# Attention and a feed-forward layer on one core: float32r scores by 64-row products on two row halves

## The chip, the cores and the metric

The kernel runs on one core of a Trainium2 chip. The metric is the device time of one execution in microseconds. Five engines work side by side, each on its own queue in order: TensorE (PE, with weight loads as PEld), VectorE (DVE), ScalarE (ACT), GpSimd (POOL) and SyncE (SP, which issues most DMAs here). They wait for each other by semaphores.

## The reference

Eight batches of eight heads, 576 positions, 64 lanes a head. Each head's scores get a bias from a running sum, a causal mask and a softmax; then a feed-forward layer runs over the 512 joined lanes of all 4608 tokens. All is float32 (q and k are drawn with a spread of 0.8, v of 0.1, s of 0.5).

```python
scores = (1 / np.sqrt(64)) * np.matmul(q, k.transpose(0, 1, 3, 2))
cum = np.cumsum(np.maximum(s, 0.0), axis=-1)
bias = -(cum[:, :, :, None] - cum[:, :, None, :])
scores = np.where(causal, -1000000000.0, scores + np.minimum(bias, 0.0))
attn = np.exp(scores - max); attn = attn / (sum(attn) + 1e-09)
x = np.matmul(attn, v)            # heads side by side: 4608 x 512
h = x @ w_in                      # 512 x 2048
g = np.where(h >= 1, h, np.where(h <= -1, 0.0, (h + 1) ** 2 / 4))
out = g @ w_out                   # 2048 x 512
```

## The kernel before

**Jobs.** Attention goes in 64 jobs: `jobs` runs over 8 batches, the two halves of the query positions (`HALF`: 320 and 256 positions), and four pairs of heads. A job takes two heads. Its query rows are tiles `QT`: 64, 128 and 128 rows in the first half (tiles 0, 1, 2, which see 64, 192 and 320 keys), 128 and 128 in the second (tiles 3, 4, which see 448 and 576; tile 4 goes in two column halves of 288). `att_slot(j, k)` emits a job in eight slots k. Between the slots the main loop emits `ffn_step`: for each half batch, 16 times twelve h products (`ffn_h`, L594, 128x320 or 128x256, f16) and twelve y products (`ffn_y`, L633). A scheduler then orders each engine's instructions by a model of its own, within the order that data, buffers and priorities ask for; the slots set the rank of the work.

**Scores.** The first 12 jobs (`F32_JOBS`, "whole" jobs) use float32 products (L432). Their operands hold 64 lanes of a head and four more rows: the running sum `cum` in two parts and constants, so that the bias comes out of the product itself (68 rows, `KC`). The 52 jobs from the 13th on (24 first halves, 28 second halves) use float32r, which keeps fewer bits, so each operand is split in two parts. The operands are four tiles, one copy each: `Q1s` and `K1s` have 128 rows, `Q2s` and `K2s` 68. `rq` and `rk` are loaded twice, into rows 0 to 63 and 64 to 127. `att_prep`, at slot 0 of the job itself, lets ACT round them (L387, L388, L389) and DVE subtract (L390, L391), and ACT's queue load `cum`'s parts into `Q2s` and `K2s` (L381, L382). Per tile, head and column half, `scores` then makes a product over 128 rows (L435) and one over 68 rows (L436) into the same bank `s` (pool `ps_s`, two banks, which `px` uses too).

**Behind the scores.** DVE adds the mask and takes the row minimum in one instruction (L441, PSUM to the tile `p`), ACT takes the exponential (L452), DVE the reciprocal of the sum (L494, L495), POOL, ACT and DVE split the weights in two f16 parts `pb` (L499 to L505), and an SP DMA transposes them into `pt`. A job later, `att_out` multiplies them with v (L535, 128 rows by 64 columns, the two heads on the two column halves of the array), and ACT and DVE make the f16 parts of x. Once a batch, L121 spreads a scale: a product with one row and one column of data.

Of the kernel before, what the change touches and what calls it, by code (L numbers as in the profile page):

```python
# [22 lines left out]
P = 128  # L23
# [54 lines left out]
def attention_ffn(ctx: ExitStack, tc: tile.TileContext, qT, kT, vn, s, w_in, w_out, yT):  # L78
# [269 lines left out]
    def att_load(n, hf):  # L348

        b, h0 = n // NPAIR, 2 * (n % NPAIR)  # L350
        q0, N, _ = HALF[hf]
        W = q0 + N
        if whole(n, hf):
            for t, src, c0 in zip(operands(n, hf), (qT, kT), (q0, 0)):
                sv = src[b, h0:h0 + 2, :, c0:W].rearrange("h d n -> d h n")
                (FIRSTQ if jobs.index((n, hf)) < FIRST_N else LOADQ).dma_start(t[:D, :, :W - c0], sv)
            return
        rq = ap.tile([P, 2, N], F32, tag="rq", bufs=1, name=f"rq{n}_{hf}")
        rk = ap.tile([P, 2, W], F32, tag="rk", bufs=1, name=f"rk{n}_{hf}")
# [4 lines left out]
        raws[n, hf] = rq, rk

    def att_prep(n, hf):
# [4 lines left out]
        if not whole(n, hf) and not split_tiles:  # L371
            split_tiles.extend(operand_tiles(F32R, "s"))
            constant_rows(*split_tiles[1])
        Qc, Kc = operands(n, hf) if whole(n, hf) else split_tiles[1]
# [8 lines left out]
        if whole(n, hf):  # L383
            return
# [4 lines left out]
        A.copy(Q2[:D, :, :N], rq[:D])  # L389
        V.tensor_tensor(Q1[D:, :, :N], rq[D:], Q1[D:, :, :N].bitcast(F32), ALU.subtract)  # L390
        V.tensor_tensor(K2[:D, :, :W], rk[:D], K1[:D, :, :W].bitcast(F32), ALU.subtract)  # L391
# [24 lines left out]

    def scores(n, i, hd, c0, c1):

        off, R, W = QT[i]
        qo = off - HALF[i // 3][0]  # L420
        if hd == 0 and c0 == 0:
            sums[n, i] = ap.tile([P, 2], F32, tag="sm", bufs=4, name=f"sm{n}_{i}")
            pbs[n, i] = []
        if c0 == 0:
            Pt = ap.tile([P, SP], F32, tag="p", bufs=4, name=f"p{n}_{i}_{hd}")
            pbs[n, i].append(Pt)
            G.memset(Pt[:R, W:W + D], 0.0)
# [1 line left out]
        sc = ps_s.tile([P, 512], F32, tag="s", name=f"s{n}_{i}_{hd}_{c0}")
        if whole(n, i // 3):  # L430
            Q, K = operands(n, i // 3)
            T.matmul(sc[:R, :c1 - c0], Q[:KC, hd, qo:qo + R], K[:KC, hd, c0:c1], start=True, stop=True)  # L432
        else:
# [1 line left out]
            T.matmul(sc[:R, :c1 - c0], Q1[:, hd, qo:qo + R], K1[:, hd, c0:c1], start=True, stop=False)  # L435
            T.matmul(sc[:R, :c1 - c0], Q2[:KC, hd, qo:qo + R], K2[:KC, hd, c0:c1], start=False, stop=True)  # L436
        mn = mins.pop((n, i, hd), None)
        m2 = ap.tile([P, 1], F32, tag="mn", bufs=6, name=f"mn{n}_{i}_{hd}_{c0}")
        mo = 448 - off + c0
        with tc.high_priority(offset=TTR_LEAD):  # L440
            ttr[0] = V.tensor_tensor_reduce(  # L441
                out=Pt[:R, c0:c1], in0=sc[:R, :c1 - c0], in1=mask[:R, mo:mo + c1 - c0],
                scale=-0.125, scalar=3.0e38 if mn is None else mn[:R],
                op0=ALU.add, op1=ALU.min, accum_out=m2[:R],
            ).ins
# [320 lines left out]
```

## Time and profile before

| | |
|---|---|
| three runs | 1098.88, 1101.65, 1103.4 us, median 1101.65 |
| profiled execution | 1098.98 us, span 1097.2 us, mean granted TensorE clock 0.984 |
| busy PE, PEld | 1014.7 us (92%), 779.6 us (71%) |
| busy DVE, ACT, POOL | 862.9 us (79%), 722.7 us (66%), 657.8 us (60%) |
| score products of the split jobs | L435 118.1 us (x312), L436 96.2 us (x312) |
| DMA | 140.33 MB, 128 GB/s on average |

Times of one instruction run from its start to its modelled end. PE's products overlap: a stream of 320-column products has one every 0.136 us though each lasts 0.30. So a sum of busy times says how long PE was occupied, and the price of a product is read from the starts of its neighbours. "Idle before" is the time that an engine stood still before an instruction, with the one that released it.

### The profile page before, as it was taken

How to read it: one execution, taken by the hardware profiler on the slowest of the kernel's cores; microseconds unless marked ns; L12 is line 12 of the kernel's file. 1: busy time of each engine (PE TensorE's matmuls, PEld its weight loads, DVE VectorE, ACT ScalarE, POOL GpSimd, SP SyncE). 2: the span in 40 equal slices, each digit the busy share in tenths (PEclk: the TensorE clock that was granted, in tenths of full speed). 3: DMA queues.
4: the chain of work that ended last, by engine and by line, in shares of the span. 5: the costliest groups of instructions: out<-in, count | busy, mean ns of one | idle time of the engine just before them, and what ended most of it. 6: DMA issues, size and time to landing. Idle time of an engine off the chain costs nothing. (4 is left out here: it accounts for less than half of the span.)

```text
span 1097.2 us, 25029 instructions
## 1 busy us (share of the span) xinstructions
PE 1014.7 (92%) x8494; PEld 779.6 (71%) x8494; DVE 862.9 (79%) x2379; ACT 722.7 (66%) x1707; POOL 657.8 (60%) x1139
## 2 busy tenths in 40 slices
PE   1567898999999999999999999899999999999998
PEld 0334566687778877787778877787777877887787
DVE  7998986678788878788788778787888888887533
ACT  4867683567567765877577765776577765777432
POOL 2843486666567656666567665666566666765522
PEclk9998999799999999999999999999999999999999
DMA  8835245546357763777366753766276753677300
GB/s 241 240 119 172 77 101 112 124 107 167 92 116 164 133 145 87 161 143 151 88 146 144 160 124 84 160 134 166 71 161 131 154 127 73 153 137 139 68 25 20
DMA packets 300839, 140.33 MB, mean 128 GB/s; under 512 B 237608, under 2 KB 286632, under 8 KB 300712
## 3 DMA queue, kind: packets, MB, share of 16 engines
q1 hardware_dynamic: 291008, 128.80, 52.2%
q10 hardware_dynamic: 9704, 9.93, 3.2%
q8 instruction: 67, 1.10, 0.4%
q14 instruction: 60, 0.49, 0.1%
HBM read 71.00 MB, written 9.73 MB: 74 GB/s over the span
## 5 line engine op out<-in xcount | busy, mean ns | idle before, releaser
L594 PE MATMUL h<-x,WI 128*128 128x256 f16 (+1 forms) x3072 | 461.4, 290 | 11.9 <-DVE u L610 7.8
L633 PE MATMUL y<-g,WO 128*128 128x256 f16 (+1 forms) x3072 | 446.2, 287 | 1.9 <-ACT g L620 1.9
L594 PEld LDWEIGHTS <-WI 128*128 128x128 f16 x3072 | 287.9, 99 | 105.0 <-issue 22.1
L633 PEld LDWEIGHTS <-WO 128*128 128x128 f16 x3072 | 288.0, 98 | 85.4 <-issue 5.7
L621 POOL TENSOR_TENSOR g<-u,g 128x320 f16<-128x320 f32 (+1 forms) x256 | 207.0, 808 | 172.0 <-ACT g L620 164.0
L452 ACT ACTIVATE p<-p,mn 64x64 f32<-64x64 f32 (+4 forms) x320 | 179.4, 561 | 118.3 <-DVE mn L441 84.6
L606 ACT ACTIVATE u<-h,ub,us 128x320 f32<-128x320 f32 (+1 forms) x256 | 149.3, 583 | 131.8 <-PE h L594 130.0
L609 DVE SCALAR_TENSOR_TENSOR h<-h,ws,u 128x320 f32<-128x320 f32 (+1 forms) x256 | 132.8, 519 | 87.7 <-ACT u L606 84.1
L499 POOL TENSOR_SCALAR pb<-p,rs 128x256 f16<-128x256 f32 (+4 forms) x148 | 94.1, 636 | 142.1 <-DVE rs L495 88.7
L502 POOL TENSOR_TENSOR pb<-p,pb 128x256 f16<-128x256 f32 (+4 forms) x148 | 156.0, 1054 | 9.8
L441 DVE CUSTOM_DVE_ANT_0 p<-s,mask 64x64 f32<-64x64 f32 (+4 forms) x320 | 134.8, 422 | 34.2 <-PE s L436 21.6
L505 DVE SCALAR_TENSOR_TENSOR pb<-p,rs,pb 128x256 f16<-128x256 f32 (+4 forms) x148 | 127.8, 864 | 22.3 <-POOL pb L499 21.7
L610 DVE SCALAR_TENSOR_TENSOR u<-u,r,h 128x320 f32<-128x320 f32 (+1 forms) x256 | 130.5, 510 | 7.4
L435 PE MATMUL s<-K1s,Q1s 128*128 128x288 f32 (+4 forms) x312 | 118.1, 379 | 10.1 <-DVE Q1s L390 5.0
L500 ACT ACTIVATE p<-p,rs 128x192 f32<-128x192 f32 (+4 forms) x148 | 84.2, 569 | 51.5 <-DVE rs L495 49.2
L620 ACT CAST g<-u 128x320 f16<-128x320 f32 (+1 forms) x256 | 108.1, 422 | 6.5 <-DVE u L610 6.3
L501 POOL TENSOR_SCALAR pb<-p 128x256 f16<-128x256 f32 (+4 forms) x148 | 87.6, 592 | 16.7 <-ACT p L500 12.6
L436 PE MATMUL s<-K2s,Q2s 68*128 68x288 f32 (+4 forms) x312 | 96.2, 308 | 0.1
L535 PEld LDWEIGHTS <-vt 128*64 128x64 f16 x1464 | 68.5, 112 | 19.9 <-issue 14.0
L535 PE MATMUL px<-pt,vt 128*64 128x256 f16 (+3 forms) x1464 | 77.2, 257 | 2.7 <-DMA pt<-pb 2.6
L435 PEld LDWEIGHTS s<-K1s,Q1s 128*128 128x128 f32 (+1 forms) x312 | 56.7, 182 | 19.5 <-PE s L436 4.5
L391 DVE TENSOR_TENSOR K2s<-rk,K1s 64x1152 fp32r<-64x1152 f32 (+1 forms) x52 | 62.9, 1209 | 5.9 <-ACT K1s L388 5.1
(134 smaller groups left out, 1034.8 us busy)
## 6 DMA issues: line engine op xcount, KB each, us to landing
rk<-in_k_dram SPq DMA_DIRECT2D x56, 288.0 KB
wir<-in_moe_w_in_dram SPq DMA_DIRECT2D x16, 512.0 KB
v<-in_v_dram SPq DMA_DIRECT2D x32, 256.0 KB
wor<-in_moe_w_out_dram SPq DMA_DIRECT2D x16, 512.0 KB
rk<-in_k_dram SPq DMA_DIRECT2D x48, 160.0 KB
rq<-in_q_dram SPq DMA_DIRECT2D x48, 160.0 KB
rq<-in_q_dram SPq DMA_DIRECT2D x56, 128.0 KB
out_dram<-o ACTq DMA_DIRECT2D x32, 160.0 KB
```

The lines of the kernel that those rows point to most:

```text
L435: T.matmul(sc[:R, :c1 - c0], Q1[:, hd, qo:qo + R], K1[:, hd, c0:c1], start=True, stop=False)
L441: ttr[0] = V.tensor_tensor_reduce(out=Pt[:R, c0:c1], in0=sc[:R, :c1 - c0], in1=mask[:R, mo:mo + c1 - c0], scale=-0.125, scalar=3.0e38 if m ...
L452: A.activation(Pt[:R, :W], Pt[:R, :W], AF.Exp, bias=m2[:R], scale=-1.0, accum_out=sums[n, i][:R, hd:hd + 1])
L502: G.tensor_tensor(los[1], pw, his[1], ALU.subtract)
L505: V.scalar_tensor_tensor(los[0], pv, rs[:R, :1], his[0], ALU.mult, ALU.subtract)
L535: T.matmul(px[hd * D:(hd + 1) * D, lo:N], vts[n][:, vl, j, hd * D:(hd + 1) * D], PT[:, 4 * j + 2 * hd + pl, lo:], start=(m == 0), stop=(m ...
L594: T.matmul(h[:, :N], WI[4 * kt + ft // 4][:, wl, ft % 4 * P:(ft % 4 + 1) * P], x[:, kt, xl], start=(n == 0), stop=(n == 3 * NKT - 1),)
L606: first = A.activation(u, h[:, :N], AF.Relu, bias=ubi[b], scale=usc[b]).ins
L609: V.scalar_tensor_tensor(h[:, :N], h[:, :N], wsc[b], u, ALU.mult, ALU.max)
L610: V.scalar_tensor_tensor(u, u, r, h[:, :N], ALU.min, ALU.mult)
L621: G.tensor_tensor(g[:, 1], u, g[:, 0], ALU.subtract)
L633: T.matmul(ys[b, hf, m][:, :N], WO[8 * (m // 2) + ft // 2][:, wl, c0:c0 + P], g[:, gl], start=(ft == 0 and n == 0), stop=(ft == NFT - 1 an ...
```

## The change

From the 13th job on, the two heads of a job lie on rows 0 to 63 and 64 to 127 of one operand tile, so q and k are loaded once. `att_split` makes the high part (ACT, L393 and L394) and the low part (DVE) of q and k at slot 3 of the job before, into one of two sets of tiles in turn. `score_pair` makes three products over 64 rows for each tile and head (high by high, low by high, high by low; L508), alternating between the heads, that is between the upper and the lower row half of the array. It does so for a group of tiles at a time (`PAIRS`): tiles 0 and 1 in one bank, tile 2, tile 3, and tile 4's two halves, hence two groups in a first-half job and three in a second-half job, 132 in all. The running sum no longer goes through the product: `bias_load` spreads `cum` of both heads over all partitions by DMA from ACT's queue (L407), POOL adds the causal mask to the diagonal block (`bias_mask`, L414), and DVE's reduction (now L456) reads that tile in place of the mask. The signs of the constant rows and of `cum` are turned round.

```diff
+PAIRS = (
+    {2: [(0, 0, QT[0][2]), (1, 0, QT[1][2])], 5: [(2, 0, QT[2][2])]},
+    {2: [(3, 0, QT[3][2])], 4: [(4, 0, S // 2)], 6: [(4, S // 2, S)]},
+)
...
+    cumf = dp.tile([BH, S], F32, name="cumf")
+    nc.sync.dma_start(cumf, cum[:BH])
...
-        rq = ap.tile([P, 2, N], F32, tag="rq", bufs=1, name=f"rq{n}_{hf}")
-        rk = ap.tile([P, 2, W], F32, tag="rk", bufs=1, name=f"rk{n}_{hf}")
+        rq = ap.tile([P, N], F32, tag="rq", bufs=1, name=f"rq{n}_{hf}")
+        rk = ap.tile([P, W], F32, tag="rk", bufs=1, name=f"rk{n}_{hf}")
         for t, src, c0 in ((rq, qT, q0), (rk, kT, 0)):
-            sv = src[b, h0:h0 + 2, :, c0:W].rearrange("h d n -> d h n")
-            for d0 in (0, D):
-                (FIRSTQ if jobs.index((n, hf)) < FIRST_N else LOADQ).dma_start(t[d0:d0 + D], sv)
+            LOADQ.dma_start(t, src[b, h0:h0 + 2, :, c0:W].rearrange("h d n -> (h d) n"))
...
-        (Q1, K1), (Q2, K2) = split_tiles
-        A.copy(Q1[:, :, :N], rq)
-        A.copy(K1[:, :, :W], rk)
-        A.copy(Q2[:D, :, :N], rq[:D])
-        V.tensor_tensor(Q1[D:, :, :N], rq[D:], Q1[D:, :, :N].bitcast(F32), ALU.subtract)
-        V.tensor_tensor(K2[:D, :, :W], rk[:D], K1[:D, :, :W].bitcast(F32), ALU.subtract)
+    def att_split(n, hf):
+        rq, rk = raws.pop((n, hf))
...
+        Q, K = parts[n, hf] = split_tiles[jobs.index((n, hf)) % 2]
+        A.copy(Q[:, 0, :N], rq)
+        A.copy(K[:, 0, :W], rk)
+        V.tensor_tensor(Q[:, 1, :N], rq, Q[:, 0, :N].bitcast(F32), ALU.subtract)
+        V.tensor_tensor(K[:, 1, :W], rk, K[:, 0, :W].bitcast(F32), ALU.subtract)
+
+    def bias_load(n, hf):
+        at, c = {}, 0
+        for i in HALF[hf][2]:
+            off, R, W = QT[i]
+            if i != 1:
+                size = 2 * S if i in (2, 4) else 2 * QT[3][2]
+                t, c = ap.tile([P, size], F32, tag=f"bc{size}", bufs=1, name=f"bc{n}_{i}"), 0
+            v = at[i] = t[:, c:c + 2 * W].rearrange("p (h w) -> p h w", h=2)
+            c += 2 * W
+            CUMQ.dma_start(v[:R], cumf[2 * n:2 * n + 2, :W].unsqueeze(0).broadcast_to([R, 2, W]))
+        biases[n, hf] = at
+
+    def bias_mask(n, i):
+        off, R, W = QT[i]
+        v = biases[n, i // 3][i]
+        tri = mask[:R, 448:448 + R].unsqueeze(1).broadcast_to([R, 2, R])
+        G.tensor_tensor(v[:R, :, off:], v[:R, :, off:], tri, ALU.add)
...
-            (Q1, K1), (Q2, K2) = split_tiles
-            T.matmul(sc[:R, :c1 - c0], Q1[:, hd, qo:qo + R], K1[:, hd, c0:c1], start=True, stop=False)
-            T.matmul(sc[:R, :c1 - c0], Q2[:KC, hd, qo:qo + R], K2[:KC, hd, c0:c1], start=False, stop=True)
...
+    def score_pair(n, hf, group):
+
+        Q, K = parts[n, hf]
+        sc = [ps_s.tile([P, 512], F32, tag="s", name=f"s{n}_{group[0][0]}_{hd}_{group[0][1]}") for hd in range(2)]
+        at, o = [], 0
+        for i, c0, c1 in group:
+            off, R, W = QT[i]
+            qo = off - HALF[hf][0]
+            at.append([t[:R, o:o + c1 - c0] for t in sc])
+            for m, (ql, kl) in enumerate(((0, 0), (1, 0), (0, 1))):
+                for hd in range(2):
+                    d = slice(hd * D, (hd + 1) * D)
+                    T.matmul(at[-1][hd], Q[d, ql, qo:qo + R], K[d, kl, c0:c1], start=(m == 0), stop=(m == 2))
+            o += c1 - c0
+        for (i, c0, c1), s2 in zip(group, at):
...
+                m2 = weights(n, i, hd, c0, c1, s2[hd], biases[n, hf][i][:R, hd, c0:c1])
...
-            if k >= 2:
-                scores(n, *UNITS[hf][k - 2])
-            if k == 3 and j + 1 < len(jobs):
+            if whole(n, hf):
+                if k >= 2:
+                    scores(n, *UNITS[hf][k - 2])
+            else:
+                for i, c0, c1 in PAIRS[hf].get(k + 1, ()):
+                    if c0 == 0:
+                        bias_mask(n, i)
+                if k in PAIRS[hf]:
+                    score_pair(n, hf, PAIRS[hf][k])
+            if k == 3 and j + 1 < F32_JOBS:
                 att_load(*jobs[j + 1])
...
+            if F32_JOBS - 1 <= j < len(jobs) - 1 and k == 3:
+                att_split(*jobs[j + 1])
+                if j + 2 < len(jobs):
+                    att_load(*jobs[j + 2])
+            if F32_JOBS - 1 <= j < len(jobs) - 1 and k == 7:
+                bias_load(*jobs[j + 1])
```

`weights` is the reduction cut out of `scores`. The scheduler's order moves with this. On PE before, in the second half of pair 9, tile 4 of its first head (names are `s_tile_head_column`, h is a product of L594, y of L633):

```order
L633 MATMUL y_1_3_4256<-g_1_12_4859,WO_141 128x256
L435 MATMUL s_4_0_0_4962<-K1s,Q1s 128x288
L436 MATMUL s_4_0_0_4962<-K2s,Q2s 128x288
L594 LDWEIGHTS WI_110
L594 MATMUL h_0_1_5142<-x_0_4073,WI_110 128x320
...
L435 MATMUL s_4_0_288_4988<-K1s,Q1s 128x288
L436 MATMUL s_4_0_288_4988<-K2s,Q2s 128x288
```

The two products of a head stand together, and h and y products fill the time to the next. On PE in the changed kernel, the same job, second column half of tile 4 (h is now L673, y L712; x3 is three products in a row):

```order
L712 MATMUL y_1_3_4338<-g_1_12_4925,WO_142 128x256
L508 MATMUL s_4_0_288_5081<-K2s,Q2s 128x288 x3
L673 LDWEIGHTS WI_115
L673 MATMUL h_1_15_5103<-x_1_3149,WI_115 128x256
...
L508 MATMUL s_4_1_288_5082<-K2s,Q2s 128x288 x3
L673 LDWEIGHTS WI_119
L673 MATMUL h_1_15_5103<-x_1_3149,WI_119 128x256
```

The first head's three products and the second head's three, alternating in the code, stand apart with h products between them. On PE in the changed kernel, the next job (pair 10), the same tile and columns:

```order
L712 MATMUL y_0_2_5327<-g_0_0_5185,WO_136 128x320
L508 MATMUL s_4_0_288_5341<-K1s,Q1s 128x288
L508 MATMUL s_4_1_288_5342<-K1s,Q1s 128x288
L508 MATMUL s_4_0_288_5341<-K1s,Q1s 128x288
L508 MATMUL s_4_1_288_5342<-K1s,Q1s 128x288
...
L673 LDWEIGHTS WI_120
```

Here the heads alternate as the code has them. On ACT before, at a job's start, the split and the loads of the sums among exponentials (L452) and the feed-forward's u and g (L606, L620):

```order
L452 ACTIVATE p_4_0_6735,sm_4_6734<-p_4_0_6735,mn_4_0_288_6766 128x576
L387 CAST Q1s<-rq_1_6716 128x2x256
L388 CAST K1s<-rk_1_6717 128x1152
L381 DMA Q2s<-cumd 2x2x256
L606 ACTIVATE u_1_14_6997<-h_1_14_6984,ub_4606,us_4602 128x256
L620 CAST g_1_12_6874<-u_1_13_6933 128x256
L452 ACTIVATE p_4_1_6781,sm_4_6734<-p_4_1_6781,mn_4_1_288_6810 128x576
L382 DMA K2s<-cumd 2x2x576
L389 CAST Q2s<-rq_1_6716 64x2x256
```

On ACT in the changed kernel, the split of pair 21's first half and a load of pair 20's bias, in the last tile of pair 19 (L474 is the exponential, L699 g):

```order
L699 CAST g_0_8_9852<-u_0_8_9853 128x320
L394 CAST K2s<-rk_0_9661 128x320
L393 CAST Q2s<-rq_0_9660 128x320
L474 ACTIVATE p_4_1_9689,sm_4_9684<-p_4_1_9689,mn_4_1_288_9759 128x576
L407 DMA bc_2_9792<-cumf 128x2x320
L616 ACTIVATE x_1_9299<-px_1_9794,shares_wi 128x256
```

Two short casts stand in place of three long ones, more than a job before their use, and the load of tile 2's bias stands before the job that uses it begins.

More of the change, by code (lines that the diff above doesn't have):

```diff
@@ L370, in att_prep @@
         cd = cumd[2 * n:2 * n + 2].rearrange("h l n -> l h n")
[L371 to L374, printed above, removed]
+        Qc, Kc = operands(n, hf)
         if jobs.index((n, hf)) < CH_N:
@@ L382, in att_prep @@
             CUMQ.dma_start(Kc[D + 2:D + 4, :, :W].bitcast(F32), cd[:, :, :W])
[L383 to L384 removed]
+    def att_split(n, hf):
         rq, rk = raws.pop((n, hf))
[L386 to L391 removed]
+        q0, N, _ = HALF[hf]
+        W = q0 + N
+        if not split_tiles:
+            split_tiles.extend(operand_tiles(F32R, "s"))
+        Q, K = parts[n, hf] = split_tiles[jobs.index((n, hf)) % 2]
[19 more added lines that the diff above has]
+        G.tensor_tensor(v[:R, :, off:], v[:R, :, off:], tri, ALU.add)
     def v_prep(n):
@@ L408, in v_low @@
                 V.scalar_tensor_tensor(VT[:, 1], v, r, VT[:, 0], ALU.mult, ALU.subtract)
-    vbs = {}
+    vbs, parts, biases = {}, {}, {}
     ttr = [None]
@@ L415, in attention_ffn, with row_tiles, row_tile, weights @@
     mins = {}
-    def scores(n, i, hd, c0, c1):
-        off, R, W = QT[i]
[L420 to L427, printed above, removed]
-        Pt = pbs[n, i][hd]
[L429 to L433, printed above, removed]
-            (Q1, K1), (Q2, K2) = split_tiles
-            T.matmul(sc[:R, :c1 - c0], Q1[:, hd, qo:qo + R], K1[:, hd, c0:c1], start=True, stop=False)
-            T.matmul(sc[:R, :c1 - c0], Q2[:KC, hd, qo:qo + R], K2[:KC, hd, c0:c1], start=False, stop=True)
+    def row_tiles(n, i):
+        sums[n, i] = ap.tile([P, 2], F32, tag="sm", bufs=4, name=f"sm{n}_{i}")
+        pbs[n, i] = []
+    def row_tile(n, i, hd):
+        R, W = QT[i][1:]
+        Pt = ap.tile([P, SP], F32, tag="p", bufs=4, name=f"p{n}_{i}_{hd}")
+        pbs[n, i].append(Pt)
+        G.memset(Pt[:R, W:W + D], 0.0)
+    def weights(n, i, hd, c0, c1, sc, bias):
+        off, R, W = QT[i]
+        Pt = pbs[n, i][hd]
         mn = mins.pop((n, i, hd), None)
         m2 = ap.tile([P, 1], F32, tag="mn", bufs=6, name=f"mn{n}_{i}_{hd}_{c0}")
-        mo = 448 - off + c0
         with tc.high_priority(offset=TTR_LEAD):
             ttr[0] = V.tensor_tensor_reduce(
-                out=Pt[:R, c0:c1], in0=sc[:R, :c1 - c0], in1=mask[:R, mo:mo + c1 - c0],
+                out=Pt[:R, c0:c1], in0=sc, in1=bias,
                 scale=-0.125, scalar=3.0e38 if mn is None else mn[:R],
@@ L445, in scores, with take_late @@
             ).ins
+        return m2
+    def take_late():
         if late:
@@ L448, in scores, with weights_end @@
                 late.pop(0)()
+    def weights_end(n, i, hd, c1, m2):
+        R, W = QT[i][1:]
         if c1 < W:
@@ L456, in scores @@
             weights_t(n, i)
+    def scores(n, i, hd, c0, c1):
+        off, R, W = QT[i]
+        qo = off - HALF[i // 3][0]
+        if hd == 0 and c0 == 0:
+            row_tiles(n, i)
+        if c0 == 0:
+            row_tile(n, i, hd)
+        sc = ps_s.tile([P, 512], F32, tag="s", name=f"s{n}_{i}_{hd}_{c0}")
+        Q, K = operands(n, i // 3)
+        T.matmul(sc[:R, :c1 - c0], Q[:KC, hd, qo:qo + R], K[:KC, hd, c0:c1], start=True, stop=True)
+        mo = 448 - off + c0
+        m2 = weights(n, i, hd, c0, c1, sc[:R, :c1 - c0], mask[:R, mo:mo + c1 - c0])
+        take_late()
+        weights_end(n, i, hd, c1, m2)
+    def score_pair(n, hf, group):
[3 more added lines that the diff above has]
+        for i, c0, c1 in group:
+            off, R, W = QT[i]
+            qo = off - HALF[hf][0]
[6 more added lines that the diff above has]
+        for (i, c0, c1), s2 in zip(group, at):
+            R = QT[i][1]
+            if c0 == 0:
+                row_tiles(n, i)
+            for hd in range(2):
+                if c0 == 0:
+                    row_tile(n, i, hd)
+                m2 = weights(n, i, hd, c0, c1, s2[hd], biases[n, hf][i][:R, hd, c0:c1])
+                if hd:
+                    take_late()
+                weights_end(n, i, hd, c1, m2)
     def plain_t(n, i):
@@ L560, in att_slot @@
             n, hf = jobs[j]
-            if k == 0:
+            if whole(n, hf) and k == 0:
                 att_prep(n, hf)
```

10 lines of the change are left out of this document (7 added, 3 removed).

## The prediction

> **What bounds the kernel now.** I read the page first: span, busy time by engine, slices.
>
> ```profile
> span 1097.2 us, 25029 instructions
> PE 1014.7 (92%) x8494; PEld 779.6 (71%) x8494; DVE 862.9 (79%) x2379; ACT 722.7 (66%) x1707; POOL 657.8 (60%) x1139
> PE   1567898999999999999999999899999999999998
> PEclk9998999799999999999999999999999999999999
> ```
>
> The profiled execution took 1098.98 us, 1.8 us around its span and 2.7 us below the median of the three runs, 1101.65; I sum against 1098.98. After the fifth slice or so PE stands at 9 everywhere and at its full clock. The split jobs, which the change rewrites, all lie there. So next come the sums from 150 us on, and what PE waited for in that stretch (nine rows, 21.3 us together; the first two and the last).
>
> ```profile
> 150.00:1097.00 947.00, 921.51 (x8086) 725.21 (x8084) 729.78 (x2007) 621.51 (x1500) 583.97 (x1027) 0.99 0.56 122
> PE s L435 <- DVE Q1s L390: 5.0, 5, 1.2
> PE s L435 <- DVE mn L441: 4.0, 6, 0.7
> ...
> PE row_m L111 <- DVE mt L293: 0.5, 1, 0.5
> ```
>
> PE is busy 921.5 of 947 us, DVE 730, ACT 622, POOL 584, the DMA engines 56%. PE is the bound and has some 21 us of waits to give back. A busy PE overlaps its own products, so I price them by starts, from the timeline. The second column is the time from the first start to the last modelled end; the ends are not used.
>
> ```profile
> 500.50 1.67 PE L594 MATMUL h<-x,WI 128*128 128x320 f16 x11
> 501.89 0.40 PE L435 MATMUL s<-K1s,Q1s 128*128 128x288 f32 x1
> 502.13 0.30 PE L436 MATMUL s<-K2s,Q2s 68*128 68x288 f32 x1
> 502.27 0.31 PE L594 MATMUL h<-x,WI 128*128 128x320 f16 x1
> 502.42 1.47 PE L633 MATMUL y<-g,WO 128*128 128x256 f16 x12
> ```
>
> Eleven 320-column products end 1.67 us after the first start, and one alone takes 0.31: ten starts in 1.36, so 0.136 us from start to start, 2.35 columns a ns. From 500.50 to 502.42 lie twelve of them (1.63) and one head's pair of score products: 0.29 for 288 columns, the late start of the product behind included. The same subtraction gives the other widths:
>
> ```profile
> 552.91 0.86 PE L594 MATMUL h<-x,WI 128*128 128x320 f16 x5
> ...
> 553.69 0.86 PE L594 MATMUL h<-x,WI 128*128 128x320 f16 x5
> ...
> 555.48 0.57 PE L594 MATMUL h<-x,WI 128*128 128x320 f16 x3
> ...
> 556.09 0.99 PE L594 MATMUL h<-x,WI 128*128 128x320 f16 x6
> 447.43 1.25 PE L633 MATMUL y<-g,WO 128*128 128x320 f16 x8 [0.21 <-ACT g L620]
> ...
> 448.80 0.72 PE L633 MATMUL y<-g,WO 128*128 128x320 f16 x4
> ...
> 513.89 0.72 PE L594 MATMUL h<-x,WI 128*128 128x320 f16 x4
> ...
> 514.85 0.45 PE L633 MATMUL y<-g,WO 128*128 128x320 f16 x2
> ```
>
> That is 0.10 for the 64-column pair, 0.20 for 192, 0.28 for 320, 0.42 for 448. Here the window stops at the product behind, which itself runs 10 to 20 ns over; I take 0.11, 0.22, 0.29, 0.30 and 0.42 for 64, 192, 288, 320 and 448 columns. One product is half of that. A first-half job (two heads, tiles 0 to 2) costs 2 x 0.63 = 1.26 us of PE, a second-half job 2 x 1.00 = 2.00; 24 and 28 split jobs make 86.2 us.
>
> **The change, on PE.** Per tile and head two products over 128 and 68 rows become three over 64 rows. Done two heads at a time on the two row halves, that would be three prices for two heads in place of four. Whether halves run side by side is seen for column halves:
>
> ```profile
> 507.02 0.84 PE L594 MATMUL h<-x,WI 128*128 128x320 f16 x5
> 507.79 1.51 PE L535 MATMUL px<-pt,vt 128*64 128x256 f16 x30
> 509.24 0.58 PE L633 MATMUL y<-g,WO 128*128 128x320 f16 x3
> 300.87 0.71 PE L594 MATMUL h<-x,WI 128*128 128x320 f16 x4
> 301.51 0.17 PE L121 MATMUL col_m<-t_m,ones 1*128 1x1 bf16 x1
> 301.61 0.40 PE L435 MATMUL s<-K1s,Q1s 128*128 128x288 f32 x1
> ```
>
> Thirty products (two halves, 15 steps of 256, 192 and 64 columns, 3072 columns a half) take 1.45 us, and 3072 columns at 2.35 a ns are 1.31: halves do run together. But the rows also show a price for going to a part of the array and back. Five h products end their turn at 507.02 + 0.68 = 507.70 and px starts at 507.79: 0.09 late. L121 uses one row of the array and one column of data. It starts at 301.51, where 300.87 + 4 x 0.136 = 301.41 was due, and the full-height product behind it starts 0.10 after it, for a product that streams one column. So a visit to a part of the rows costs 0.10 in and 0.10 out here; I take 0.195.
>
> No row has 64 rows visited from a full PE. The Trainium skill ("TensorEngine Tiling (Array Packing)", Key Properties) says that a change of tiling mode drains TensorE, whichever the mode; by that rule 64 rows pay as one row does, which is the value that I take from L121.
>
> After the drain the first weight load is in the open. Its length by the rows:
>
> ```profile
> L435 PEld LDWEIGHTS s<-K1s,Q1s 128*128 128x128 f32 x264 | 50.1, 190 | 10.6 <-PE s L436 4.5
> ...
> L435 PEld LDWEIGHTS s<-K1s,Q1s 128*64 128x64 f32 x48 | 6.5, 136 | 8.8 <-ACT g L620 3.4 <-ACT x L552 2.9 <-ACT Q2s L389 1.5
> ...
> L633 PEld LDWEIGHTS <-WO 128*128 128x128 f16 x3072 | 288.0, 98 | 85.4 <-issue 5.7
> ```
>
> Sixty-four more columns take 54 ns more, so a load occupies 0.11 us for 128 columns and 0.055 for 64.
>
> What decides is how often the array changes, and the changed order on PE says it. I counted stretches of L508 rows (the new score product): 232, where 132 groups are written in the code. Only 40 stretches hold both heads; 192 hold one, with h and y products between the first head's three and the second's. Products by price: 85 stretches of three 288-column products (3 x 0.145), 37.0 us; 43 of 448 (3 x 0.21), 27.1; 33 of 64 and 192 columns (3 x 0.165), 16.3; 16 of 320 (3 x 0.15), 7.2; the 40 with both heads, 20.8 (one price for two heads where the rows alternate, more where they stand three and three); 15 broken ones, 3.9. Together 112.3 us. Visits: 232 x 0.195 = 45.2; loads in the open, 188 x 0.11 + 44 x 0.055 = 23.1; less 17 stretches next to px or L121, which share a switch, 1.7. After: 178.9 us against 86.2, **+92.7 us**. Bounds of the unknown part: a visit at nothing gives +26.1; at 0.30 in place of 0.195, as if the drain were half as long again, +117.
>
> **The other parts.** The split stands a job ahead on two sets of tiles, so PE's waits for Q1s (5.0 us) and others behind ACT's casts go; with PE slower the other waits shrink too. Of the 21.3 us I take 8 back; ends 0 and 21. ACT loses one cast of three and half the elements of the others; DVE subtracts half the elements. Both only add slack (they have 325 and 217 us of it), and what stands behind them on ACT's queue (exp, u, g) comes earlier, not later. The score reduction L441 reads a bias tile in place of the mask, same size, nothing.
>
> New on POOL: 128 masks of up to 128x2x128 floats, in order with the g differences that y products need. Nearest row:
>
> ```profile
> L502 POOL TENSOR_TENSOR pb<-p,pb 128x256 f16<-128x256 f32 x28 | 20.9, 746 | 1.8
> ...
> DMA packets 300839, 140.33 MB, mean 128 GB/s; under 512 B 237608, under 2 KB 286632, under 8 KB 300712
> ```
>
> 128 x 0.75 = 96 us on an engine with 363 idle: nothing on the path while POOL's idle covers it; without that cover g would be late, y next. Data: a first-half job loads 320 KB of q and k in place of 640 KB, and 544 KB of bias; a second-half job 416 in place of 832, and 1024. Net 24 x 224 + 28 x 608 KB = 22 MB on 140, with DMA engines at 56%: nothing, hidden by a lead of about half a job or more in ACT's queue. The loads stand behind exps on ACT and wait for the reductions that free the bias tile; ACT's slack hides their issue. The first 12 jobs keep their products; one more small DMA of 144 KB at the start, 0 to 1 us.
>
> Sum: 1098.98 + 92.7 - 8 = **1184 us**, 7.5% above the median.
>
> **Rivals.**
> *Visits cost nothing* for 64 rows: loads go ahead under the running product and nothing drains. For it: full-height loads do lie under products (98 ns each, one every 0.11 us). Against: both part-array cases above pay each time. It leaves +26.1 to +49 (loads in the open) less 8: 1117 to 1140.
> *Not slower*: the same, and the earlier split and the lighter ACT and DVE give back all 21.3 us of PE's waits. Then 1099 + 26.1 - 21.3 = 1104, no change. It decides only if a visit costs under 0.015 us (3 us over 232), and the separated heads keep it from going below.
> *Weights of the same rows not hidden*: within a visit of one head, the second and third load wait for the running product. Some 2.5 such loads a visit at 0.1 us: 232 x 0.25 = +58, 1242. Against: L633 loads the same rows while they work, and stays at 0.109 a product. The Trainium skill ("TensorE: Matmul & The Clock Gate", Part 3, What overlaps) says that a load overlaps a running product only where its row group differs; by that rule it would be 1242, and the trace's full-height rows disagree.
> *Bias late*: a second-half job's 1 MB comes at what the DMA engines have free, 0.44 x 128/0.56 = 100 GB/s, in 10 us of the job's 17. If it is late by 2 us in 28 jobs, the two score banks stay held and PE stops in order: +56, 1240.
>
> **How the numbers follow.** Chances: forecast 0.79; visits free 0.07; not slower 0.04; weights not hidden 0.05; bias late 0.05. The forecast's own ends: all 21 us given back and the load hidden, 1147; the longer drain, 1208. That holds 8 in 10, so the range is 1148 to 1208. A measurement of this kernel can tell about 0.5%. Slower by more than that: all but the second rival and a little, 0.96; same 0.03; faster 0.01.
>
> **What would show it.** PEld idle of about 0.26 us put down to issue, as before px, ahead of some 230 score visits; L508 products of one head starting 0.145 (288 columns) to 0.21 apart; the alternating stretches with two heads starting together; PE busy above 1090 us, its waits from 150 us on under 20 us. Wrong would be: h and y products 0.136 apart right up to L508 and after it (visits free), loads in L508 one after another with gaps (weights), or PE idle before L508 released by POOL or DVE (bias).

## The result, and the profile after

The changed kernel takes 1209.33 us, median of four runs (1208.33 to 1216.6), against 1101.51 for the kernel before: a ratio of 1.1004 [1.0976, 1.1032]. The prediction was 1184 with a range of 1148 to 1208. The direction was right, the time 25 us too short, just outside the range. The profiled execution is the one of 1216.6 us, 7.3 above the median; where I sum by the trace, I sum against it.

The page of the changed kernel: span, busy time by engine, PE's forty slices, and two groups (busy time, mean ns of one, idle time before them and its releaser).

```profile
span 1214.4 us, 25380 instructions
PE 1108.3 (91%) x8806; PEld 806.9 (66%) x8806; DVE 828.8 (68%) x2379; ACT 667.7 (55%) x1655; POOL 706.4 (58%) x1265
PE   2656997999998999989998999999999999999998
L712 PE MATMUL y<-g,WO 128*128 128x256 f16 (+1 forms) x3072 | 442.9, 288 | 23.6 <-POOL g L700 20.1
L414 POOL TENSOR_TENSOR bc<-bc,mask 128x256 f32<-128x256 f32 (+1 forms) x128 | 92.4, 722 | 81.1 <-DMA bc<-cumf 78.8
```

PE is busy 94 us longer, above the 1090 us that the prediction named as a sign, and DVE, ACT and POOL stay far from full, as forecast. But PE's row has three 8s between its thirteenth and its twenty-second slice, where the kernel before has 9s, and POOL stood still for 81 us ahead of the new masks. Next the sums from 150 us on, PE's longest waits there, and three of POOL's (engine, line, what it waited for: us, times, longest). The last row is the kernel before.

```profile
150.00:1214.00 1064.00, 1016.47 (x8386) 751.27 (x8383) 700.50 (x2008) 565.06 (x1446) 631.23 (x1150) 0.98 0.56 129
PE y L712 <- POOL g L700: 20.1, 21, 3.1
PE px L599 <- DMA pt<-pb: 6.3, 9, 1.3
PE h L673 <- DVE u L689: 3.8, 3, 1.5
```

```profile
POOL bc L414 <- DMA bc<-cumf: 66.5, 60, 4.9
POOL p L448 <- DVE pb L569: 51.9, 61, 2.7
POOL pb L563 <- DMA pt<-pb: 47.2, 22, 3.9
...
POOL pb L499 <- DMA pt<-pb: 12.8, 12, 2.4
```

PE's waits from 150 us on are 43.8 us (idle times summed), where the kernel before had 21.6 and the prediction 13. The largest is new: y products wait for g from POOL. Such a wait in the timeline, on ACT's queue, POOL and PE; POOL's stop here is the longest of the 60 ahead of masks:

```profile
532.92 0.34 ACTq L407 DMA_DIRECT2D bc<-cumf  x1
```

```profile
535.37 0.80 POOL L563 TENSOR_SCALAR pb<-p,rs 128x640 f16<-128x640 f32 x1 [0.77 <-DVE rs L559]
541.09 0.73 POOL L414 TENSOR_TENSOR bc<-bc,mask 128x256 f32<-128x256 f32 x1 [4.92 <-DMA bc<-cumf]
541.78 1.32 POOL L565 TENSOR_SCALAR pb<-p 128x640 f16<-128x640 f32 x1
543.07 0.66 POOL L700 TENSOR_TENSOR g<-u,g 128x256 f16<-128x256 f32 x1
```

```profile
540.87 0.72 PE L712 MATMUL y<-g,WO 128*128 128x256 f16 x5
543.78 1.14 PE L712 MATMUL y<-g,WO 128*128 128x256 f16 x7 [2.19 <-POOL g L700]
```

The bias load is issued at 532.92 and lands at about 541.0. POOL, which takes its instructions in order, stands 4.92 us before the mask; the split L565 and the g difference behind it come late, and PE stands 2.19 us. The bias itself is in no hurry there: over all loads, matched with the reductions that read them, the load is issued 0.1 us after its tile came free, POOL is ready for the mask 3.9 us after the issue, the mask starts 4.66 us after it (medians), and the first reduction of that tile 11.4 to 14.0 us after it (medians by tile).

This is the rarer kind. For each of the 21 waits for g I looked for POOL's longest stop in the 9 us before that g was ready: a mask's wait for its load in 3 of them (3.5 of the 20.1 us), and in 17 (13.4 us) L563, the first instruction of the weights' split, which waits until a transposition (`pt`, by DMA) has read the tile `pb`. One of those, on SP's and ACT's queues, POOL and PE:

```profile
510.29 2.16 SPq L570 DMA_TRANSPOSE pt<-pb  x1
510.67 0.40 ACTq L407 DMA_DIRECT2D bc<-cumf  x1
516.39 0.48 POOL L563 TENSOR_SCALAR pb<-p,rs 128x256 f16<-128x256 f32 x1 [2.95 <-DMA pt<-pb]
517.37 0.76 POOL L700 TENSOR_TENSOR g<-u,g 128x256 f16<-128x256 f32 x1
518.18 1.14 PE L712 MATMUL y<-g,WO 128*128 128x256 f16 x9 [0.89 <-POOL g L700]
```

A bias load follows the transposition by 0.4 us, and POOL stands 2.95 us until the transposition is done.

What score products cost, by starts, for one head (448 columns) and for both heads at once (288):

```profile
536.45 1.47 PE L712 MATMUL y<-g,WO 128*128 128x256 f16 x12
537.85 0.87 PE L508 MATMUL s<-K2s,Q2s 64*128 64x448 f32 x3
538.65 1.48 PE L673 MATMUL h<-x,WI 128*128 128x256 f16 x12
...
530.19 0.60 PE L712 MATMUL y<-g,WO 128*128 128x256 f16 x4
530.72 0.66 PE L508 MATMUL s<-K1s,Q1s 64*128 64x288 f32 x6
531.32 1.05 PE L673 MATMUL h<-x,WI 128*128 128x256 f16 x8
```

Twelve 256-column products take 1.31 us, so the one-head visit costs 538.65 - 537.76 = 0.89 (0.907 with the late start behind; the forecast had 0.63 + 0.195 + 0.11 = 0.935). The two-head visit costs 0.69. One head alone with 288 columns costs the same, 0.699 at the median of 85.

I applied the same counting to every stretch of score products and in every run: from the start of the product ahead of it to the second start behind it, less the f16 products' own time (0.109 and 0.136 us) and less idle time. "Rest" is the last product's start less the two columns before it.

| kernel | score visits (both heads) | score products, us | PE's waits from 150 us | rest | median of the runs |
|---|---|---|---|---|---|
| before | full height | 94.9 | 21.6 | 976.3 | 1101.51 |
| changed | 232 (40) | 179.7 | 43.8 | 986.5 | 1209.33 |
| bias loaded twice only | 241 (34) | 180.9 | 14.0 | 975.0 | 1177.21 |
| masks left out | 240 (30) | 183.5 | 22.1 | 978.6 | 1190.61 |
| mask one tile later | 245 (19) | 193.3 | 41.4 | 978.5 | 1223.47 |
| mask a little later | 259 (5) | 199.2 | 13.3 | 971.7 | 1188.84 |
| full height | 232, full height | 136.8 | 56.6 | 985.3 | 1183.56 |
| full height, mask one tile later | 245, full height | 145.6 | 66.1 | 980.1 | 1194.40 |
| full height, mask a little later | 259, full height | 140.1 | 25.3 | 974.9 | 1144.26 |
| heads forced together | 131 (131) | 110.8 | 144.8 | 1030.0 | 1286.04 |
| before, second product of 64 rows | 312 of one product | 175.2 | 10.6 | 973.8 | 1165.28 |

The change cost 84.8 us of score products, 22.2 of waits and 10.2 of rest, 117 in all, the difference of the two profiled executions. The growth of the rest is for the most part the granted clock. Twelve y products in a stretch at half clock (core 0: us, busy time of PE, PEld, DVE, ACT and POOL, granted clock, DMA share, GB/s):

```profile
902.70:909.50 6.80, 6.78 (x30) 4.51 (x30) 4.87 (x20) 4.85 (x17) 4.21 (x10) 0.50 0.69 143
905.47 3.41 PE L712 MATMUL y<-g,WO 128*128 128x320 f16 x12
908.67 1.92 PE L673 MATMUL h<-x,WI 128*128 128x256 f16 x12
```

They start 0.267 us apart in place of 0.136. From 150 us on such stretches add up to 47.8 us in the changed kernel, 23.9 in the kernel before and 146.8 with the heads forced together; at half rate the 23.9 us more are about 12 us of lost time, and the rest grew by 10.2. Over the eleven kernels the rest grows by 0.44 us for each us of such stretches (a fit, from 13.7 to 146.8 us).

### The profile page after: what moved, and what is told of

Same layout as the page of the kernel before. It is cut to its first block, busy times and chain, and to the rows that moved or that the text cites. A ratio compares the mean times of both kernels' runs of the same rounds, so it can differ in the third digit from the quotient of the medians.

```text
span 1214.4 us, 25380 instructions
## 1 busy us (share of the span) xinstructions
PE 1108.3 (91%) x8806; PEld 806.9 (66%) x8806; DVE 828.8 (68%) x2379; ACT 667.7 (55%) x1655; POOL 706.4 (58%) x1265
## 4 chain that ended last, share of the span: by engine, by line
PE 59%; DMA 17%; DVE 9%; POOL 6%; ACT 4%; issue 3%; DVEq 0%; ACTq 0%; POOLq 0%; SPq 0%
PE h L673 22%; PE y L712 22%; DMA pt<-pb 10%; PE s L508 9%; PE px L599 4%; DMA bc<-cumf 3%; DMA wor<-in_moe_w_out_dram 2%; DVE K2s L396 2%; DMA wir<-in_moe_w_in_dram 2%; POOL pb L563 1%; POOL pb L566 1%; PE s L490 1%; DVE p L456 1%; POOL bc L414 1%; ACT p L474 1%
## 5 line engine op out<-in xcount | busy, mean ns | idle before, releaser
L673 PE MATMUL h<-x,WI 128*128 128x256 f16 (+1 forms) x3072 | 460.5, 290 | 15.8 <-DVE u L689 12.2
L712 PE MATMUL y<-g,WO 128*128 128x256 f16 (+1 forms) x3072 | 442.9, 288 | 23.6 <-POOL g L700 20.1
L712 PEld LDWEIGHTS <-WO 128*128 128x128 f16 x3072 | 297.7, 98 | 116.7 <-issue 38.2
L673 PEld LDWEIGHTS <-WI 128*128 128x128 f16 x3072 | 288.7, 99 | 125.5 <-issue 50.1
L700 POOL TENSOR_TENSOR g<-u,g 128x320 f16<-128x320 f32 (+1 forms) x256 | 196.4, 767 | 160.7 <-ACT g L699 151.9
L474 ACT ACTIVATE p<-p,mn 64x64 f32<-64x64 f32 (+4 forms) x320 | 178.5, 558 | 171.7 <-DVE mn L456 160.9
L456 DVE CUSTOM_DVE_ANT_0 p<-s,bc 128x448 f32<-128x448 f32 (+4 forms) x256 | 107.9, 433 | 110.1 <-PE s L508 67.1
L563 POOL TENSOR_SCALAR pb<-p,rs 128x256 f16<-128x256 f32 (+4 forms) x148 | 89.2, 603 | 129.6 <-DMA pt<-pb 47.2
L566 POOL TENSOR_TENSOR pb<-p,pb 128x256 f16<-128x256 f32 (+4 forms) x148 | 143.2, 968 | 5.5
L414 POOL TENSOR_TENSOR bc<-bc,mask 128x256 f32<-128x256 f32 (+1 forms) x128 | 92.4, 722 | 81.1 <-DMA bc<-cumf 78.8
L689 DVE SCALAR_TENSOR_TENSOR u<-u,r,h 128x320 f32<-128x320 f32 (+1 forms) x256 | 130.7, 511 | 9.6
L569 DVE SCALAR_TENSOR_TENSOR pb<-p,rs,pb 128x256 f16<-128x256 f32 (+4 forms) x148 | 115.6, 781 | 23.3 <-POOL pb L563 22.9
L699 ACT CAST g<-u 128x320 f16<-128x320 f32 (+1 forms) x256 | 107.6, 420 | 10.9 <-DVE u L689 10.5
L508 PE MATMUL s<-K2s,Q2s 64*128 64x288 f32 (+4 forms) x468 | 89.6, 322 | 0.1
L599 PEld LDWEIGHTS <-vt 128*64 128x64 f16 x1464 | 69.3, 112 | 25.3 <-issue 19.9
L565 POOL TENSOR_SCALAR pb<-p 128x256 f16<-128x256 f32 (+4 forms) x148 | 81.1, 548 | 5.6 <-ACT p L564 4.8
L448 POOL MEMSET p<- 128x64 f32 (+1 forms) x320 | 46.5, 151 | 64.3 <-DVE pb L569 52.5
L508 PE MATMUL s<-K1s,Q1s 64*128 64x288 f32 (+4 forms) x468 | 79.7, 327 | 0.2 <-DVE x L617 0.2
```

The source lines that it names most:

```text
L456: ttr[0] = V.tensor_tensor_reduce(out=Pt[:R, c0:c1], in0=sc, in1=bias, scale=-0.125, scalar=3.0e38 if mn is None else mn[:R], op0=ALU.add, ...
L474: A.activation(Pt[:R, :W], Pt[:R, :W], AF.Exp, bias=m2[:R], scale=-1.0, accum_out=sums[n, i][:R, hd:hd + 1])
L508: T.matmul(at[-1][hd], Q[d, ql, qo:qo + R], K[d, kl, c0:c1], start=(m == 0), stop=(m == 2))
L566: G.tensor_tensor(los[1], pw, his[1], ALU.subtract)
L569: V.scalar_tensor_tensor(los[0], pv, rs[:R, :1], his[0], ALU.mult, ALU.subtract)
L599: T.matmul(px[hd * D:(hd + 1) * D, lo:N], vts[n][:, vl, j, hd * D:(hd + 1) * D], PT[:, 4 * j + 2 * hd + pl, lo:], start=(m == 0), stop=(m ...
```

## The experiments

**The bias loaded twice only.** Theory: POOL in order stands before a late bias load. In this kernel the tiles are loaded for the first job of each half and kept, so later jobs have a wrong bias; products and masks stay.

```diff
-                t, c = ap.tile([P, size], F32, tag=f"bc{size}", bufs=1, name=f"bc{n}_{i}"), 0
+                if size not in keep:
+                    keep[size] = ap.tile([P, size], F32, tag=f"bc{size}", bufs=1, name=f"bc{n}_{i}")
+                t, c = keep[size], 0
...
+            if (n, hf) in jobs[F32_JOBS:F32_JOBS + 1] + jobs[16:17]:
...
```

> The changed kernel with each bias tile loaded once for the first job that uses it and kept (later jobs get a wrong bias); POOL still adds its 128 masks. Theory (POOL stands in order behind late bias loads, and g and so y behind POOL): POOL's waits for bias loads go from 66 us to about 0, PE's waits for g from 20 us to under 5, time 1209 - 20 = 1185 to 1190. Rival (POOL's 92 us of masks themselves delay g): waits stay, 1205 to 1213. Second rival (PE's waits come from the scheduler's order, whatever is late): PE's waits for POOL stay above 15 us.

Measured: 1177.21 us, ratio to the kernel before 1.0708 [1.0684, 1.0731], 32 us less than the changed kernel and 8 below the theory's range. PE's wait for g in this kernel, and the masks:

```profile
PE y L715 <- POOL g L703: 3.6, 8, 0.8
L417 POOL TENSOR_TENSOR bc<-bc,mask 128x256 f32<-128x256 f32 (+1 forms) x128 | 122.5, 957 | 108.9 <-DVE mn L459 91.3 <-DMA bc<-cumf 16.7 <-DVE u L692 0.9
```

POOL spends 122.5 us on its masks, more than the 92.4 of the changed kernel, and stands still for 108.9 us ahead of them, for the most part until a reduction lets go of the tile; the score products cost as before, and the 20.1 us have become 3.6. So neither the masks' work nor the sum of POOL's stops before them is the price. About 30 us of the change hang on the loads, and the rest of the forecast stands without them (1184 forecast, 1177 measured). It leaves open whether the loads hurt by their traffic or by the place of the wait.

**Full height.** All 936 score products take 128 rows instead of 64, so that the array isn't changed (the scores are then sums over both heads).

```diff
-                    d = slice(hd * D, (hd + 1) * D)
+                    d = slice(0, P)
```

> The changed kernel with every score product over all 128 rows (both heads' lanes are multiplied and summed, so the scores are the sum of the two heads'). Same 936 products and weight loads, no change of the array's shape. Theory (drain and open load of each visit are the price): 3 x 0.315 x 2 x 24 + 3 x 0.50 x 2 x 28 = 129 us in place of 174, so 45 us less: about 1164, with products 0.14 apart at 288 columns and no idle weight loads ahead of them. Rival (three products for two is the price, visits are free): no change, 1205 to 1213.

Measured: 1183.56 us, ratio 1.0768 [1.0736, 1.08]; 26 us gained, not 45. The one-head visit of 448 columns:

```profile
524.15 1.47 PE L712 MATMUL y<-g,WO 128*128 128x256 f16 x12
525.38 0.85 PE L508 MATMUL s<-K2s,Q2s 128*128 128x448 f32 x3
526.08 1.49 PE L673 MATMUL h<-x,WI 128*128 128x256 f16 x12
```

It takes 526.08 - 525.46 = 0.62 where 64 rows took 0.89, a price of 0.27 for going to half the rows and back; the medians give 0.284 (448 columns), 0.287 (288), 0.288 (320) and, away from px products, 0.233 (64 and 192). The forty visits with both heads lose by full height (288 columns: 0.815 in place of 0.699), so scores fall by 43 us only. And 13 us of that came back as waits (56.6 in place of 43.8), 2.0 of them for g and 4.2 for u (L689).

**The kernel before, with 64 rows in its second product.** This is the price alone, without any other part of the change (the bias rows are left out).

```diff
-            T.matmul(sc[:R, :c1 - c0], Q2[:KC, hd, qo:qo + R], K2[:KC, hd, c0:c1], start=False, stop=True)
+            T.matmul(sc[:R, :c1 - c0], Q2[:D, hd, qo:qo + R], K2[:D, hd, c0:c1], start=False, stop=True)
```

> The kernel before with one edit: the second product of each pair takes 64 rows in place of 68 (the bias rows are left out). Less data, same 624 products, but 312 visits to half the rows. Theory (0.195 us of drain and 0.107 of open weight load a visit, 0.053 where 64 columns are loaded): 264 x 0.30 + 48 x 0.25 = 91 us more, 1185 to 1193. Rival (64 rows cost nothing special): 1101.

Measured: 1165.28 us, ratio 1.0592 [1.0571, 1.0613], 65 us more for four rows fewer. Two heads of 288 columns:

```profile
510.98 0.93 PE L633 MATMUL y<-g,WO 128*128 128x256 f16 x7
511.66 0.38 PE L435 MATMUL s<-K1s,Q1s 128*128 128x288 f32 x1
511.97 0.40 PE L436 MATMUL s<-K2s,Q2s 64*128 64x288 f32 x1
512.30 0.72 PE L633 MATMUL y<-g,WO 128*128 128x256 f16 x5
```

The pair takes 512.30 - 511.74 = 0.56 where the kernel before took 0.29. Over all widths the score products cost 175.2 us in place of 94.9, 0.26 for each of 312 visits; 11 us come back from PE's waits. The expectation used 0.30 a visit and gave nothing back, hence its 20 to 28 us too much.

**Heads forced together.** The two score banks become one tile of two banks, so that both heads' products start together.

```diff
-    ps_s = ctx.enter_context(tc.tile_pool(name="ps_s", bufs=2, space=PSUM))
+    ps_s = ctx.enter_context(tc.tile_pool(name="ps_s", bufs=1, space=PSUM))
...
-        sc = [ps_s.tile([P, 512], F32, tag="s", name=f"s{n}_{group[0][0]}_{hd}_{group[0][1]}") for hd in range(2)]
+        both = ps_s.tile([P, 2, 512], F32, tag="s", name=f"s{n}_{group[0][0]}_{group[0][1]}")
+        sc = [both[:, hd] for hd in range(2)]
...
```

> The changed kernel with the two score banks handed out as one pair, so that a group's products can only start when both heads have a bank: 131 visits to 64 rows in the order, all with both heads, in place of 232 of which 40 have both. Theory (a visit costs the same for one head as for two, 0.70 us at 288 columns, 0.91 at 448, 0.75 to 0.79 in the first half): score visits fall from 174 us to 24 x 1.53 + 28 x 2.31 = 101, so 73 us less: about 1136, up to 1150 if the single pair of banks makes new waits. Rival (the cost is the 936 products themselves, and putting heads side by side saves nothing): 1209.

Measured: 1286.04 us, ratio 1.1704 [1.167, 1.1738]. The visits did what was expected: 131, and score products of 110.8 us, 69 less. The time went the other way. Px and the first twelve jobs' scores (L490) share those banks, and only one tile is left:

```profile
PE px L600 <- DMA pt<-pb: 42.3, 13, 4.9
PE y L713 <- POOL g L701: 37.2, 33, 3.0
PE s L509 <- DVE mn L456: 16.4, 20, 1.4
PE px L600 <- DVE mn L456: 13.9, 15, 2.2
PE s L490 <- DVE mn L456: 9.0, 15, 0.7
```

The last three rows, 39 us, are waits for a reduction that empties the tile. How px's wait for the transposed weights and y's for g follow from the single tile was not traced, and the granted clock was 0.93 on average. So it shows what a visit costs, not what the pairing would be worth: it changed a second thing, and that was larger.

**The mask one tile later.** Now to tell POOL's wait from traffic: same loads, same masks, but each mask is ordered behind the last weight instruction (L566 of the changed kernel) that is written ahead of it.

```diff
...
-        G.tensor_tensor(v[:R, :, off:], v[:R, :, off:], tri, ALU.add)
+        with tc.issue_after(behind[0]):
+            G.tensor_tensor(v[:R, :, off:], v[:R, :, off:], tri, ALU.add)
...
-        G.tensor_tensor(los[1], pw, his[1], ALU.subtract)
+        behind[0] = G.tensor_tensor(los[1], pw, his[1], ALU.subtract).ins
```

> Same loads of the bias, same masks on POOL, same score products; the mask stands one or two instructions later on POOL, behind the weights' last instruction of a tile. In the changed kernel a bias load is issued 0.05 to 0.1 us after its tile comes free, the mask stands 4.7 us behind the issue at the median, the load lands after 4.2 to 4.7 us, and the first reduction that reads the tile comes only 11 to 14 us after the issue. Theory (POOL in order waits for a load that is late for the mask, not for the reduction): POOL's wait before the mask falls from 66 us to under 20, PE's wait for g from 20 us to under 6, time 1178 to 1192. Rival (the traffic of the loads slows the other transfers): POOL's wait may fall, but the transposed weights stay late, 1200 to 1213. Rival (POOL's own 92 us of masks): no change, 1203 to 1213.

Measured: 1223.47 us, ratio 1.1114 [1.1077, 1.1151]: all three readings missed the time. As the theory has it, POOL's wait for the load is gone (0.0 us in its group) and PE's wait for g falls to 2.9 us, but the mask now starts 13.4 us after the issue at the median, and the reduction waits for it:

```profile
L417 POOL TENSOR_TENSOR bc<-bc,mask 128x256 f32<-128x256 f32 (+1 forms) x128 | 97.8, 771 | 0.0
```

```profile
DVE p L459 <- POOL bc L417: 85.5, 66, 3.8
```

The mask had moved by a whole tile, past the time at which it is needed. The order on PE moved as well, to 19 visits with both heads, which cost 14 us of the score products.

**Masks left out.** The loads stay, nothing on POOL waits for them (the diagonal blocks keep what a mask would remove).

```diff
-        G.tensor_tensor(v[:R, :, off:], v[:R, :, off:], tri, ALU.add)
```

> The masks on POOL are left out (the diagonal blocks keep scores that a mask would remove); the bias loads stay as they are. Theory (a load late only for POOL's mask): the reductions need the tile 11 to 14 us after the issue, so nothing waits, 1172 to 1185. Rival (traffic): 1200 to 1213. Rival (POOL's own work): also 1172 to 1185; the run with the masks set later tells it from the theory.

Measured: 1190.61 us, ratio 1.081 [1.0773, 1.0847], 19 us less than the changed kernel and 6 outside the theory's range. PE's waits fall to 22.1, y's for g to 11.5. About 13 us remain to the run without loads. Traffic has a part in them: POOL's stops at the split for transpositions stay at 47.4 us (47.2 in the changed kernel, 9.2 with the bias loaded twice only), and they are its longest stop ahead of 10 of PE's 12 waits for g (8.2 us). By the trace's DMA packets, tile 4's transposition takes 5.4 us here from its issue to its last packet, 5.1 in the changed kernel, 3.7 without the loads (medians). But the traffic alone does not set PE's waits: the run after the next has the loads, a transposition of 5.2 us, the masks, and waits of 13.3.

**Full height and the mask one tile later.** An edit of both kinds, meant to add two gains.

> Score products over 128 rows in place of 64 (scores are then the sum over both heads) and the mask set later, together. Theory (two separate terms, the visits to 64 rows and POOL's wait for the bias): the full-height change alone gave 1183.6 with PE's waits at 56.6 us; with those down to 15 to 20 it is 1143 to 1152. Rival (a third term, such as the traffic or DVE): 1160 or more.

Measured: 1194.4 us, ratio 1.0833 [1.0801, 1.0864], with PE's waits at 66.1 us and 100 us of DVE waiting for the mask. The rival's number; the third term is DVE's wait for the mask, not DVE's own work or the traffic.

**The mask a little later.** The same edit, one tile earlier: each mask is ordered behind the last weight instruction but one that is written ahead of it. "The last run" in the next text is the run with the mask one tile later.

```diff
...
-        with tc.issue_after(behind[0]):
+        with tc.issue_after(behind[-2]):
...
-        behind[0] = G.tensor_tensor(los[1], pw, his[1], ALU.subtract).ins
+        behind.append(G.tensor_tensor(los[1], pw, his[1], ALU.subtract).ins)
```

On POOL, in one place, changed kernel and this one:

```
L565 TENSOR_SCALAR pb_3_8878<-p_3_1_8870 128x4x128
L414 TENSOR_TENSOR bc_3_9017<-bc_3_9017,mask 128x2x128
L566 TENSOR_TENSOR pb_3_8878<-p_3_1_8870,pb_3_8878 128x4x128

L568 TENSOR_SCALAR pb_3_8878<-p_3_1_8870 128x4x128
L569 TENSOR_TENSOR pb_3_8878<-p_3_1_8870,pb_3_8878 128x4x128
L417 TENSOR_TENSOR bc_3_9017<-bc_3_9017,mask 128x2x128
```

> The mask stands on POOL behind the weights' last instruction of the tile before, one tile earlier than in the last run and one or two instructions later than in the changed kernel. In the last run the mask stood 13.4 us behind the load's issue in place of 4.7, POOL waited for no load, but 66 reductions on DVE waited for the mask, 85 us. Here I expect 6.5 to 8.5 us behind the issue. The order of PE moves too: 259 score visits, 5 with both heads, where the changed kernel has 232 and 40; by 0.75 us for a visit that is 20 to 24 us more (179.7 to 200 or 204). Theory (the bias has a window: loaded at 4.5 us, needed at 11): POOL's wait for the load under 20 us, DVE's for the mask under 25, PE's waits 12 to 20 us, time 978 + 202 + 16 + 5 = 1195 to 1207. Rival (POOL is simply too full with 92 us of masks for its place in the chain): PE's waits stay near 41 to 44, 1220 to 1235.

Measured: 1188.84 us, ratio 1.0792 [1.077, 1.0815], with nothing left out, 6 us below the theory's range. At the median the mask starts 5.56 us after the issue, earlier than expected and 0.9 later than in the changed kernel:

```profile
L417 POOL TENSOR_TENSOR bc<-bc,mask 128x256 f32<-128x256 f32 (+1 forms) x128 | 91.1, 718 | 8.9 <-DMA bc<-cumf 8.5
L715 PE MATMUL y<-g,WO 128*128 128x256 f16 (+1 forms) x3072 | 444.7, 287 | 2.8 <-POOL g L703 2.7
```

POOL's idle time before the masks falls from 81.1 to 8.9 us, PE's wait for g from 20.1 to 2.7, all of PE's waits to 13.3, which is the forecast's 13. The loads and the 91 us of masks are all there. DVE waits 30.2 us for masks, above the 25 expected. The 0.9 us is not the whole move: POOL is ready for the mask at 5.6 us in place of 3.9, and by tile the median start goes from 4.0 to 5.1 us to 4.6 to 6.0, but to 13.3 for tile 2. In the changed kernel 79 of the 128 masks stand directly behind L563 or L565, inside a split, ahead of L566, which the transposition needs; here all stand behind a split's last instruction, alone or two in a row. POOL's stops for transpositions are 26.7 us in place of 47.2. It is 20 us faster than the changed kernel although its order costs 19.5 us more of score products, 259 visits with 5 pairs.

**Full height and the mask a little later.**

> The same place of the mask, with score products over 128 rows (scores are then the sum over both heads): at full height a head apart costs no more than two heads together, so the order's 259 visits cost nothing. Theory (two terms alone, visits and the place of the mask): scores 146 us as in the run before, PE's waits 12 to 20, rest 978: 1140 to 1152. Rival (waits have another source, POOL's work or the traffic): PE's waits at 55 to 66 us as with full height before, 1183 to 1195.

Measured: 1144.26 us, ratio 1.0392 [1.0367, 1.0416], in the theory's range and 39 us from the rival's. PE's waits were 25.3 us, more than the 12 to 20 expected, the score products 6 less. Against the first full-height kernel the mask starts 0.8 us later (5.48 us after the issue in place of 4.72), and the waits are 25.3 in place of 56.6.

No version beat the kernel before. By these rows a perfect one would about break even, as an estimate: 110.8 us for 131 paired visits, 13.3 of waits and 971.7 of rest make 1095.8 against its 1092.8. The 110.8 was measured with the clock at half for part of the time; by the medians of the same visits (0.70, 0.91, 0.79 and 0.75 us) it would be 102, and the sum 1087.

## Why the prediction missed

**The score products: right.** Forecast 178.9 us, 179.7 by starts. The number of stretches (232) was in the changed order; the price of 0.195 + 0.11 (305 ns) was 0.28 to 0.29 where full height and 64 rows differ in nothing else, and 0.23 for the groups that begin with 64 columns of weights. Only the sum was measured, not its two parts. The Trainium skill ("TensorEngine Tiling (Array Packing)", Key Properties) says that a change of mode drains TensorE, and the 65 us for four rows fewer agree. The Trainium skill ("TensorE: Matmul & The Clock Gate", Part 3, What overlaps) also says that a load overlaps a running product only where the row group differs; that does not hold here. With 0.28 off the visit of 0.89, three products on the same rows take 0.61, 0.203 each, hardly over the 0.19 for which 448 columns stream. The rival *weights of the same rows not hidden*, 1242, did not come. The kernel before costs 94.9 by the same count, where the prediction had 86.2, so the term is +84.8 and not +92.7; an error of 8 us that made the forecast longer and, by luck, the miss smaller. (PE does not quite "stand at 9 everywhere" after the fifth slice, as the text reads the page: the seventh and the 26th slice show 8, and the clock's eighth shows 7. No term rests on it.)

**The step that failed: POOL's masks and the bias loads "at nothing".** The text put the masks under POOL's 363 idle us, and the loads under "a lead of about half a job or more". From a load's issue to the time at which POOL reached its mask there were 3.9 us at the median, since there is one tile of each kind and its load can't be issued before the last reduction has read it; the load needs 4.5 us at the median and 8.1 at the longest (of the 26 whose landing the profile gives). In place of -8 us PE's waits came to +22.2, with 10.2 of rest, for the most part time at half clock: 40 us from this one step, of which the profiled execution shows 1216.6 - 1184 = 32.6 after the 8 above. Without the loads waits and rest are 14.0 and 975.0, with the masks behind the split 13.3 and 971.7; so the loads and the place of the masks together are shown as the cause.

The road from there to the late g is shown only in part. A mask's wait stands directly ahead of 3.5 of the 20.1 us, a late transposition ahead of 13.4. Transpositions are late where they run beside a load (5.1 us for 3.7), and a mask inside the split puts 0.72 us of work and its own wait ahead of L566; how much each of the two did was not told apart. Idle time on an engine that works in order covers work, not a wait that stands ahead of other work; and what such a wait costs depends on what stands behind it, not on its length (108.9 us of stops before masks cost little in the run without the loads).

**The named cover was right, its test was not made.** "Without that cover g would be late, y next" is the chain that came. The rival *bias late* took another road (score banks held, 1240) and had 5 in 100. In the trace of the changed kernel most masks stand inside a split, with g differences behind it, and the single tile of each kind stood in the change; the two were not put together.

**The range.** Its upper end, 1208, was a longer drain alone. The measured time lies 1.3 us above it. The rival with the bias late, 1240, stood outside.

**The forecast without this step** was run: loads not awaited, 1177.21; mask a little later, 1188.84.

## What to carry to other kernels

Before an engine's idle time is counted as cover, look at what the new instruction waits for and what stands behind it on that engine's queue; a transfer into a single tile has for its lead only the time from the last reader to the first use. Then place the instruction between landing and need, and not inside a sequence that others wait for: behind the split it gained 20 us here, and a tile later it lost them again. A product on part of the array's rows pays for the visit, not for the rows, so it must be grouped, or be worth 0.28 us each time.

## What the runs showed of the hardware

- A visit to 64 rows costs 0.28 us with 128 columns of float32r weights (0.20 for the 64-column pair), whether it brings one product or three. Four rows fewer in one product of a pair made a kernel 65 us longer.
- Two heads on the two row halves together cost no more than one: 0.698 against 0.699 us (288 columns), 0.907 both (448). In two visits whose products do not alternate throughout, by the spacing of their starts, both heads of 64 and 192 columns took 1.19 us in place of 0.80.
- The granted clock stands at half for stretches of 3.4 to 27 us in every run, and products there start about twice as far apart (0.267 for 0.136 us at 320 columns): 23.9 us of it from 150 us on in the kernel before, 47.8 in the changed one, 146.8 with the heads forced together. What sets it off was not tested.
- A transposition by DMA takes longer beside other loads: 5.1 us in place of 3.7 for tile 4.
